# Attention in a fused kernel: the value sums with the values as weights, and the probabilities divided before they are transposed

## The chip, the cores and the metric

The kernel runs on one core of a Trainium2 chip. The metric is the device time of one execution in microseconds (us), taken as the median of several executions. A core has five engines that run side by side and wait for each other through semaphores: PE (TensorE, matrix products; its weight loads are a row of their own in the profile, PEld), DVE (VectorE), ACT (ScalarE), POOL (GpSimd) and SP (here only the queue that issues most DMAs). Each engine works through its own list of instructions strictly in order.

## The reference, cut to what matters

Windowed attention over 4 batches, 8 heads, 768 positions and head width 64, followed by a gated feed-forward layer with a spatial mixing matrix. All of it is float32.

```python
for c in range(nc):                      # 24 chunks of 32 queries
    k_full = concat([mem_k, k[l_start:r_end]])   # 8 memory keys and up to 56 neighbours
    v_full = concat([mem_v, v[l_start:r_end]])
    scores = scale * (q_c @ k_full.T)
    scores = scores - max(scores, -1)
    a = exp(scores)
    a = a / (sum(a, -1) + 1e-09)
    out[c] = a @ v_full
x = out.transpose(0, 2, 1, 3).reshape(B, S, H * D)   # 512 features
h = maximum(x @ w_in, 0.0)
u, v = h[..., :512], h[..., 512:]
v_n = (v - mean(v)) / sqrt(var(v) + 1e-06)
v_s = einsum('ts,bsd->btd', w_spatial, v_n) + b_spatial[None, :, None]
return (u * v_s) @ w_out
```

## The kernel before

**Units.** Attention is cut into 24 units. A unit is 128 query positions (four chunks `c` of 32) of one batch, for all eight heads. The heads are held as four pairs `t`; a pair's two heads `r` lie on partitions 0 to 63 and 64 to 127. Each chunk's window is 64 keys wide. One product of a unit is therefore 4 x 4 x 2 = 32 small matmuls, called a burst here; a float32 matmul shows as two LDWEIGHTS and two MATMUL records, so a burst is 64 records of each.

**One unit, step by step** (line numbers are those of the profile):

- `prep` copies the keys into `kmain` (ACT, L375).
- The scores burst writes the PSUM tile `sx` (PE, L388, in the trace `sx<-kmain,q`): weights are 64 rows by 32 queries, and 64 key columns stream through them.
- `softmax`: the maximum (DVE, L441), the subtraction into `p` (DVE, L445), the exponential (ACT, L450), then sum, epsilon and reciprocal into `rec` (DVE, L455 to L458).
- `turn`: four 128x128 transposes of the undivided `p` into PSUM tile `pt` (PE, L472), copied to `pT` (ACT, L475).
- The value burst (PE, L388, `sx<-vmain,pT`): weights are 64 keys by 32 queries of `pT`, and the 64 value columns stream. Queries come out on partitions. It writes the other half of the `sx` tile of the next unit, and from unit 6 on it is issued as one operation with the next unit's scores.
- `norm` multiplies by the reciprocals, out of PSUM, into `xs` (DVE, L424).
- `turn_x`: four 128x128 transposes of `xs` into `xt` (PE, L487), because the feed-forward layer needs features on partitions.
- `high` and `low` split `xt` into two float32r parts in the tile `x` (ACT, L492, and DVE, L496).

**Around it.** `ffn_v` (one 512-wide group for each unit) and `ffn_u` (four 384-wide groups for every three units) take `x` and the prepared `w_in` in 12 matmuls a group, three for each of four chunks `c` of 128 features (L525 to L527). The `w_in` chunks are prepared at the start from 64-bit words by `from_f64`: a load into `big`, two ACT steps (L825, L830), a DVE step (L834, L835), a POOL addition (L840), and a split on ACT (L854) with a subtraction on DVE or POOL (L858). After the last feed-forward group come the spatial and output products (L686), which the change does not touch.

**What sets the order.** `Plan` simulates all operations with costs written in the code, and emits them in the order of their planned starts. Each operation names its engine, its planned cost, the keys it reads and writes, and a rank; among operations that can start equally early the lower rank goes first. Feed-forward groups have the highest ranks, so they fill PE wherever attention is not ready. Rings (`sizes`) limit how many tiles of a kind are alive. So any edit in the attention steps can move instructions on every engine.

## Time and profile before

| quantity | value |
|---|---|
| median of three executions | 379.65 us |
| the three executions | 379.65, 381.89, 379.65 us |
| the profiled execution, its own time | 378.39 us |
| span of the profiled execution (first to last instruction) | 376.2 us |
| busy: PE, PEld | 355.6, 327.8 us |
| busy: DVE, ACT, POOL | 275.0, 188.8, 139.8 us |
| scores burst, 24 units, MATMUL records | 21.5 us busy |
| value burst, 24 units, MATMUL records | 22.8 us busy |
| transposes `pt` and `xt`, 96 matmuls each | 15.5 and 14.5 us busy |

Busy time is the union of an engine's instructions. A row of a timeline gives the start in us, the duration in us, engine, line, operation, what it writes and reads, and in brackets the idle time of the engine just ahead of it with the operation that ended it. Matmuls overlap each other, so the distance between two starts, not the duration, says what one costs.

### The profile page before, as it was taken

What the parts mean: (1) busy time and instruction counts of PE and PEld (TensorE: products, weight loads), DVE (VectorE), ACT (ScalarE), POOL (GpSimd) and SP (SyncE); (2) the same over time, 40 slices, a digit from 0 to 9 for tenths busy, and PEclk for the clock granted to TensorE, in tenths of its full rate; (3) what the DMA queues carried; (4) which work ended last, traced back from release to release, by engine and by line L of the source; (5) the groups of instructions that cost most, each with busy time, mean ns of one, the idle gap of its engine ahead of it and who ended that gap; (6) DMA issues with size and microseconds to landing.
All of it is one profiled execution on the core that took longest, in us unless ns stands there. A gap on an engine that the chain in (4) does not pass through costs nothing.

```text
span 376.2 us, 11734 instructions
## 1 busy us (share of the span) xinstructions
PE 355.6 (95%) x4964; PEld 327.8 (87%) x4964; DVE 275.0 (73%) x470; ACT 188.8 (50%) x336; POOL 139.8 (37%) x143
## 2 busy tenths in 40 slices
PE   1569899999999999999999999999999999999996
PEld 1357698898988988989889899999999999999996
DVE  3887875757767667775498589787858795896694
ACT  3757544554654456354473366327533742553371
POOL 5444652383484088510033195251026002203410
PEclk9969999999999999999999999999999999999999
DMA  8998888888786783865832649204720582140014
GB/s 230 290 233 228 186 250 232 230 234 250 218 237 192 251 232 92 264 212 181 233 142 92 216 142 319 101 0 167 250 89 0 170 257 80 61 144 8 2 44 167
DMA packets 47368, 65.12 MB, mean 173 GB/s; under 512 B 4434, under 2 KB 38866, under 8 KB 47316
## 3 DMA queue, kind: packets, MB, share of 16 engines
q1 hardware_dynamic: 46900, 64.25, 56.4%
q8 instruction: 39, 0.64, 0.7%
q10 hardware_dynamic: 416, 0.13, 0.1%
q14 instruction: 13, 0.11, 0.1%
HBM read 45.49 MB, written 18.87 MB: 171 GB/s over the span
## 4 chain that ended last, share of the span: by engine, by line
PE 91%; DVE 4%; ACT 2%; DMA 1%; issue 1%; SPq 0%; ACTq 0%; DVEq 0%
PE y L686 22%; PE f L686 17%; PE f L525 13%; PE f L526 12%; PE f L527 12%; PE sx L388 10%; PE xt L487 3%; PE pt L472 3%; DMA k<-in_k_dram 1%; DVE st L835 1%; DVE st L834 1%; DVE mx L441 1%; DVE p L445 0%; PE y L680 0%; PE f L680 0%
## 5 line engine op out<-in xcount | busy, mean ns | idle before, releaser
L742 POOL TENSOR_TENSOR ug<-st,ug 128x384 f32<-128x384 f32 x24 | 33.1, 1392 | 97.7 <-DVE st L734 97.7
L686 PE MATMUL y<-wsp,op 128*128 128x384 f32 x288 | 52.6, 336 | 0.0
L686 PEld LDWEIGHTS y<-wsp,op 128*128 128x128 f32 x288 | 50.1, 188 | 0.0
L525 PE MATMUL f<-x,win_h 128*128 128x384 f32 x128 | 46.3, 362 | 0.0
L527 PE MATMUL f<-x,win_h 128*128 128x384 f32 x128 | 43.1, 337 | 0.0
L526 PE MATMUL f<-x,win_l 128*128 128x384 f32 x128 | 43.0, 336 | 0.0
L525 PE MATMUL f<-win_h,x 128*128 128x512 f32 x96 | 41.7, 435 | 0.0
L686 PE MATMUL f<-wsp,op 128*128 128x384 f32 x216 | 40.1, 336 | 0.0
L526 PE MATMUL f<-win_h,x 128*128 128x512 f32 x96 | 38.6, 402 | 1.5 <-DVE x L496 1.5
L664 DVE TENSOR_TENSOR op<-sm,op 128x768 fp32r<-128x768 f32 x32 | 33.4, 1050 | 7.2 <-ACT op L661 6.6
L527 PE MATMUL f<-win_l,x 128*128 128x512 f32 x96 | 38.4, 400 | 0.0
L686 PEld LDWEIGHTS f<-wsp,op 128*128 128x128 f32 x216 | 37.6, 188 | 0.0
L686 PE MATMUL y<-wout,op 128*128 128x256 f32 x288 | 35.7, 280 | 0.0
L424 DVE TENSOR_TENSOR xs<-sx,rec 128x512 f32<-128x512 f32 x24 | 16.5, 689 | 25.8 <-PE sx L388 25.6
L686 PEld LDWEIGHTS y<-wout,op 128*128 128x128 f32 x288 | 34.8, 188 | 0.1
L661 ACT CAST op<-sm 128x768 fp32r<-128x768 f32 x32 | 26.3, 838 | 15.5 <-DVE sm L647 7.7
L571 POOL TENSOR_TENSOR rstd<-ve,mhalf 128x1 f32<-128x1 f32 x24 | 14.6, 610 | 52.2 <-DVE ve L567 51.8
L388 PEld LDWEIGHTS sx<-kmain,q 64*32 64x32 f32 x1536 | 17.5, 110 | 17.1 <-POOL vmain L370 9.5
L388 PE MATMUL sx<-kmain,q 64*32 64x64 f32 x1536 | 21.5, 235 | 10.6 <-ACT kmain L375 8.4
L596 ACT ACTIVATE uo<-f 128x384 f32<-128x384 f32 x32 | 15.6, 491 | 24.5 <-PE f L527 23.0
L370 POOL COPY vmain<-memv 8x1024 f32<-8x1024 f32 x22 | 23.5, 1075 | 10.2 <-PE sx L388 8.5
L686 PE MATMUL f<-wout,op 128*128 128x256 f32 x216 | 27.1, 280 | 0.0
(92 smaller groups left out, 732.8 us busy)
## 6 DMA issues: line engine op xcount, KB each, us to landing
vmain<-in_v_dram SPq DMA_DIRECT2D x48, 128.0 KB
vn_far<-st SPq DMA_DIRECT2D x24, 256.0 KB
u_far<-uo SPq DMA_DIRECT2D x32, 192.0 KB
vr<-vn_far SPq DMA_DIRECT2D x8, 768.0 KB
ug<-u_far SPq DMA_DIRECT2D x16, 384.0 KB
q<-in_q_dram SPq DMA_DIRECT2D x11, 512.0 KB
out_dram<-ot SPq DMA_DIRECT2D x36, 128.0 KB
vmain<-in_v_dram SPq DMA_DIRECT2D x47, 96.0 KB
```

Of the source, the lines that this page charges most:

```text
L370: {"DVE": nc.vector, "POOL": nc.gpsimd}[eng].tensor_copy(to, of)
L388: nc.tensor.matmul(o, w_, m, start=True, stop=True, skip_group_check=True)
L424: nc.vector.tensor_tensor(xs.rearrange("p t r d -> p r t d"), t_["sx", i][:, :, 1], rec.rearrange("p t r -> p r t").unsqueeze(3).broadcast ...
L525: nc.tensor.matmul(o, lh, rh, start=(j == 0), stop=False)
L526: nc.tensor.matmul(o, ll, rh, start=False, stop=False)
L527: nc.tensor.matmul(o, lh, rl, start=False, stop=(j == len(pairs) - 1))
L571: nc.gpsimd.tensor_tensor(a, t_["ve", i], mhalf, op=ALU.pow)
L596: op("ACT", act(HT), lambda: nc.scalar.activation(alloc("uo", i, [P, HT], F32), t_["f", n], AF.Relu), r=[("f", n)], w=[("uo", i)], rank=rank)
L661: nc.scalar.copy(half(0), of())
L664: nc.vector.tensor_tensor(half(1), of(), half(0).bitcast(F32), op=ALU.subtract)
L686: nc.tensor.matmul(o, x, y, start=first and m == 1 and not (seed and bank != "x"), stop=m == 3 * chunks, skip_group_check=True)
L742: nc.gpsimd.tensor_tensor(g, t_[st(x)], g, op=ALU.mult)
```

## The change

The order of the steps of a unit changes, and the roles of the operands in the value burst are swapped.

- `norm` now divides `p` in place, in SBUF, directly after the reciprocals (DVE), and `turn` transposes the divided `p`.
- The value burst becomes `value_sums`, an operation of its own. The 64x64 block of values is the weight, and the 32 columns of `pT` stream. The result has features on partitions and goes into `xt` directly. It is read by `high` and `low` as before.
- `turn_x`, `xs` and their ring are gone. `sx` still takes two PSUM banks, of which half is used; `xt` takes two banks instead of one, and `pt` one buffer instead of two.
- In `xt`, the head pairs with odd `t` (`e = 1`) have their two heads swapped on the partitions (`r ^ e`), so that two row groups that share output partitions write to different banks. To match it, the rows of the odd chunks of `w_in` are loaded as two swapped halves: `from_f64` now issues one DMA for each entry of a list.
- Scores and value sums are separate operations for all units. `value_sums` has the unit's rank plus 9, the ring `st` grows from 9 to 10.

```diff
-    sizes = {"f": 3, "sx": 1, "pt": 2, "xt": 1, "y": 5, "st": 9, "big": 4, "uo": 2, "x": 2, "vm": 3,
-             "q": 2, "k": 2, "kT": 2, "p": 1, "xs": 1, "pT": 1, "vr": 2, "op": 4, "sm": 2, "ug": 6, "ot": 11}
+    sizes = {"f": 3, "sx": 1, "xt": 1, "pt": 1, "y": 5, "st": 10, "big": 4, "uo": 2, "x": 2, "vm": 3,
+             "q": 2, "k": 2, "kT": 2, "p": 1, "pT": 1, "vr": 2, "op": 4, "sm": 2, "ug": 6, "ot": 11}
...
-                for t, c, r, rows in tiles:
-                    mm(sx[c * CH:(c + 1) * CH, r, 1, t], pT[rows, t, c * CH:(c + 1) * CH], vt[rows, t, c])
...
+    def value_sums(i, rank):
...
+        def go():
+            xt = alloc("xt", i, [P, 2, 2, T // 2, UT], F32, psum=True)[:, :, 0]
+            t_["xt", i] = xt
+            pT, vt = t_["pT", i], v_of(i)
+            for u, c, e, r in [(u, c, e, r) for u in range(T // 2) for c in range(UC) for e in range(2) for r in range(2)]:
+                t, rows = 2 * u + e, head_rows[r]
+                mm(xt[head_rows[r ^ e], e, u, c * CH:(c + 1) * CH], vt[rows, t, c], pT[rows, t, c * CH:(c + 1) * CH])
...
+        op("PE", 0.8, go, r=[("pT", i)] + v_keys(i), w=[("xt", i)], rank=rank, tail=0.25)
...
+        def norm():
+            p3 = t_["p", i].rearrange("p t r w -> p (t r) w")
+            nc.vector.tensor_tensor(p3, p3, t_["rec", i].unsqueeze(2).broadcast_to([P, T * 2, WIN]), op=ALU.mult)
...
-            def turn_x():
-                xs = t_["xs", j].rearrange("p t r d -> p t (r d)")
-                a = alloc("xt", j, [P, T, P], F32, psum=True)
-                for t in range(T):
-                    nc.tensor.transpose(a[:, t], xs[:, t], ident)
...
-        load(get, src_.bitcast(U32).rearrange("p (c w) -> p c w", w=2), w=[("big", big)], r=after, rank=load_rank, seq=True)
+        n = P // len(src_)
+        for j, rows in enumerate(src_):
+            load(lambda j=j: (t_[big] if big in t_ else get())[j * n:(j + 1) * n], rows.bitcast(U32).rearrange("p (c w) -> p c w", w=2),
+                 w=[("big", big, j)], r=after, rank=load_rank, seq=True)
...
-        z, zk = from_f64(("win", c, part), w_in[c * P:(c + 1) * P, cols], rank, load_rank, False)
+        z, zk = from_f64(("win", c, part), [w_in[k * D:(k + n) * D, cols] for k, n in ([(2 * c + 1, 1), (2 * c, 1)] if c % 2 else [(2 * c, 2)])], rank, load_rank, False)
```

**What moves on PE in the steady part.** In a row of the instruction order the tile written stands ahead of the arrow, then the streamed operand and the weights; `x32` counts matmuls. This is PE's list before, from the scores burst of unit 6 (the first of the second batch) to the next transposes:

```order
L388 MATMUL sx<-kmain_144,q 32x64 x32
L388 MATMUL sx<-vmain,pT 32x64 x32
L525 MATMUL f<-win_h,x 128x512
L526 MATMUL f<-win_h,x 128x512
L527 MATMUL f<-win_l,x 128x512
L525 MATMUL f<-win_h,x 128x512
L526 MATMUL f<-win_h,x 128x512
L527 MATMUL f<-win_l,x 128x512
L487 MATMUL xt<-ident,xs 128x128 x4
```

And the same place now (L503 to L505 are the former L525 to L527, L474 is the former L472):

```order
L388 MATMUL sx<-kmain_141,q 32x64 x32
L474 MATMUL pt<-ident,p 128x128 x4
L503 MATMUL f<-win_h,x 128x512
L504 MATMUL f<-win_h,x 128x512
L505 MATMUL f<-win_l,x 128x512
L503 MATMUL f<-win_h,x 128x512
L504 MATMUL f<-win_h,x 128x512
L505 MATMUL f<-win_l,x 128x512
L388 MATMUL xt<-pT,vmain 64x32 x32
L388 MATMUL sx<-kmain_142,q 32x64 x32
```

The value burst no longer follows a scores burst as one operation, and the second set of transposes is gone. From the value sums of the fourth unit to the end (21 value and 20 scores bursts), the list before has 18 scores and value bursts joined, three value and two scores bursts apart, and two sets of transposes for each unit. Now eight pairs stand next to each other, 13 value and 12 scores bursts stand apart, and there is one set of transposes for each unit. The feed-forward groups between them are the same.

**What moves on PE at the start.** Before, around the end of the first feed-forward group, units 1 and 2:

```order
L527 MATMUL f<-win_l,x 128x512
L388 MATMUL sx<-vmain,pT 32x64 x32
L472 MATMUL pt<-ident,p 128x128 x4
L388 MATMUL sx<-kmain_145,q 32x64 x32
L487 MATMUL xt<-ident,xs 128x128 x4
L388 MATMUL sx<-vmain,pT 32x64 x32
L525 MATMUL f<-win_h,x 128x512
```

Now, between the second and the third feed-forward group:

```order
L504 MATMUL f<-win_h,x 128x512
L505 MATMUL f<-win_l,x 128x512
L474 MATMUL pt<-ident,p 128x128 x4
L388 MATMUL xt<-pT,vmain 64x32 x32
L503 MATMUL f<-win_h,x 128x512
L504 MATMUL f<-win_h,x 128x512
L505 MATMUL f<-win_l,x 128x512
```

The transposes and the value burst of unit 2 have moved from ahead of the second group to behind it, and the third group, which reads unit 2's `x`, follows the value burst directly.

**What moves on ACT at that place.** Before, from the copy of unit 2's `pT` on (numbers tell tiles apart; `x_380` written from `xt_604` is unit 2's high part):

```order
L475 COPY pT_498<-pt_490 128x512
L825 ACTIVATE st_501<-big_313 128x512
L830 ACTIVATE big_313<-big_313 128x512
L492 CAST x_380<-xt_543 128x4x128
L825 ACTIVATE st_595<-big_377 128x512
L830 ACTIVATE big_377<-big_377 128x512
L854 CAST win_h_109<-st_501 128x512
L825 ACTIVATE st_616<-big_384 128x512
L830 ACTIVATE big_384<-big_384 128x512
L492 CAST x_380<-xt_604 128x4x128
```

Now, from the same copy to the same high part, which is written from `xt_569`:

```order
L477 COPY pT_561<-pt_553 128x512
L537 ACTIVATE st_567<-f_535 128x512
L812 ACTIVATE big_367<-big_367 128x512
L807 ACTIVATE st_610<-big_379 128x512
L812 ACTIVATE big_379<-big_379 128x512
L836 CAST win_h_109<-st_527 128x512
L420 CAST x_357<-xt_569 128x2x2x128
```

Five operations stand between the two now, eight before; the copy has moved behind most of the preparation of `w_in`.

More of the change, by code (lines that the diff above doesn't have):

```diff
@@ new lines, in tile_chunked_attention_gmlp, with mm, scores @@
+    head_rows = [slice(r * D, (r + 1) * D) for r in range(2)]
+    def mm(o, w_, m):
+        nc.tensor.matmul(o, w_, m, start=True, stop=True, skip_group_check=True)
+    def scores(i, rank):
+        def go():
+            sx = alloc("sx", i, [P, 2, 2, T, D], F32, psum=True)[:, :, 0]
+            t_["sx", i] = sx
+            tq = q_of(i)
+            kT = kmain[i % NK].rearrange("p t c s -> p t (c s)")
+            for t, c, r in [(t, c, r) for t in range(T) for c in range(UC) for r in range(2)]:
+                mm(sx[c * CH:(c + 1) * CH, r, t], tq[head_rows[r], t, c * CH:(c + 1) * CH],
+                   kT[head_rows[r], t, c * SLOT:c * SLOT + WIN])
+        op("PE", 0.8, go, r=qk_keys(i, "q") + [("kmain", i % NK), ("kmem", i % NK)], w=[("sx", i)], rank=rank, tail=0.25)
@@ new lines, in value_sums, with go, part, high @@
+    def value_sums(i, rank):
+        b, tt = i // UB, i % UB
+        n, o = 2 * b + tt // HU, (tt % HU) * UT
+        def go():
+            xt = alloc("xt", i, [P, 2, 2, T // 2, UT], F32, psum=True)[:, :, 0]
[4 more added lines that the diff above has]
+                mm(xt[head_rows[r ^ e], e, u, c * CH:(c + 1) * CH], vt[rows, t, c], pT[rows, t, c * CH:(c + 1) * CH])
+        def part(l):
+            return t_["x", n][:, l].rearrange("p (u e) m -> p e u m", e=2)[:, :, :, o:o + UT]
+        def high():
+            if ("x", n) not in t_:
+                alloc("x", n, [P, 2, T, HT], F32R)
+            nc.scalar.copy(part(0), t_["xt", i])
+        def low():
+            nc.vector.tensor_tensor(part(1), t_["xt", i], part(0).bitcast(F32), op=ALU.subtract)
+        op("PE", 0.8, go, r=[("pT", i)] + v_keys(i), w=[("xt", i)], rank=rank, tail=0.25)
+        op("ACT", act(512) - 0.04, high, r=[("xt", i)], w=[("x", n, tt, "h")], rank=rank)
+        op("DVE", dve(512), low, r=[("xt", i), ("x", n, tt, "h")],
+           w=[("x", n, tt, "l"), *(["attended"] if i == NU - 1 else [])], rank=rank)
@@ new lines, in softmax, with turn, go, copy @@
+        op("DVE", dve(512), sub, r=[("sx", i), ("mx", i)], w=[("p", i)], rank=rank)
+        op("ACT", act(512), exp, w=[("p", i)], rank=rank)
+        op("DVE", dve(512) + 0.43, den, r=[("p", i)], w=[("rec", i)], rank=rank, shared=True)
+        op("DVE", dve(512), norm, r=[("rec", i)], w=[("p", i)], rank=rank, shared=True)
+    def turn(i, rank):
+        def go():
+            p = t_["p", i].rearrange("p t r w -> p t (r w)")
+            a = alloc("pt", i, [P, T, P], F32, psum=True)
+            for t in range(T):
+                nc.tensor.transpose(a[:, t], p[:, t], ident)
+        def copy():
+            nc.scalar.copy(alloc("pT", i, [P, T, P], F32), t_["pt", i])
+        op("PE", 0.47, go, r=[("p", i)], w=[("pt", i)], rank=rank, tail=0.25)
+        op("ACT", act(512) - 0.04, copy, r=[("pt", i)], w=[("pT", i)], rank=rank)
@@ L970, in tile_chunked_attention_gmlp @@
         spread_keys(j, 1.0 + j)
[L971 to L972 removed]
+    for i in range(NU):
+        attend(i, 10.0 * i)
         if i == 0:
```

107 lines of the change are left out of this document (19 added, 88 removed).

## Prediction

> **What bounds the kernel now.** I read the page first, from it the busy shares and the chain of work that ended last:
>
> ```profile
> span 376.2 us, 11734 instructions
> PE 355.6 (95%) x4964; PEld 327.8 (87%) x4964; DVE 275.0 (73%) x470; ACT 188.8 (50%) x336; POOL 139.8 (37%) x143
> PEclk9969999999999999999999999999999999999999
> PE 91%; DVE 4%; ACT 2%; DMA 1%; issue 1%; SPq 0%; ACTq 0%; DVEq 0%
> ```
>
> PE is busy 95% of the span and carries 91% of the chain; its granted clock is full but for the third slice. So the first question is where PE is idle. The windows (stretch, its length, busy time of each engine with the count of records, granted clock, DMA share, GB/s) tell it:
>
> ```profile
> 0.00:20.00 20.00, 7.49 (x204) 5.32 (x204) 12.75 (x22) 10.48 (x18) 10.48 (x16) 1.00 0.98 264
> 20.00:30.00 10.00, 7.19 (x116) 5.46 (x116) 7.64 (x16) 5.24 (x10) 2.91 (x2) 0.66 0.97 238
> 30.00:40.00 10.00, 7.99 (x203) 5.98 (x188) 9.11 (x16) 8.19 (x15) 5.86 (x6) 1.00 0.81 221
> 40.00:80.00 40.00, 39.97 (x816) 35.11 (x815) 28.99 (x60) 20.31 (x37) 20.17 (x22) 1.00 0.83 220
> ```
>
> From 40 us to the last products PE never stops, whatever DVE, ACT or DMA do. There, the time changes only by what PE itself has to execute. PE is idle for 376.2 - 355.6 = 20.6 us; 12.5 + 2.8 + 2.0 = 17.3 of them lie ahead of 40 us, where units 0 to 2 run as a chain over all engines, and the rest at the end. So the sum has two terms: PE work removed or added after the start, at its full price, and the shift of the moment from which PE no longer stops.
>
> **Term 1: PE in the steady part.** What an attention step costs there is not its busy time but the delay of the feed-forward matmuls around it. In the timeline, one set of transposes:
>
> ```profile
> 44.12 0.33 PE L526 MATMUL f<-x,win_l 128*128 128x384 f32 x1
> 44.29 0.34 PE L527 MATMUL f<-x,win_h 128*128 128x384 f32 x1
> 44.47 0.60 PE L487 MATMUL xt<-ident,xs 128*128 128x128 f32 x4
> 44.82 0.42 PE L525 MATMUL f<-x,win_h 128*128 128x384 f32 x1
> 45.08 0.34 PE L526 MATMUL f<-x,win_l 128*128 128x384 f32 x1
> ```
>
> Two 384-wide starts are normally 0.17 apart. From 44.29 to 45.08 are 0.79 for two of them: the transposes cost 0.79 - 0.34 = 0.45 us. A value burst alone, and one joined with scores:
>
> ```profile
> 41.50 0.40 PE L527 MATMUL f<-win_l,x 128*128 128x512 f32 x1
> 41.82 0.86 PE L388 MATMUL sx<-vmain,pT 64*32 64x64 f32 x64
> 42.61 0.50 PE L525 MATMUL f<-win_h,x 128*128 128x512 f32 x1
> 42.95 0.39 PE L526 MATMUL f<-win_h,x 128*128 128x512 f32 x1
> ...
> 56.91 0.40 PE L526 MATMUL f<-win_h,x 128*128 128x512 f32 x1
> 57.14 0.40 PE L527 MATMUL f<-win_l,x 128*128 128x512 f32 x1
> 57.47 0.86 PE L388 MATMUL sx<-kmain,q 64*32 64x64 f32 x64
> 58.13 0.96 PE L388 MATMUL sx<-vmain,pT 64*32 64x64 f32 x64
> 59.35 0.40 PE L526 MATMUL f<-win_h,x 128*128 128x512 f32 x1
> ```
>
> Two 512-wide starts are 0.23 apart. Alone: 42.95 - 41.50 - 0.46 = 0.99 us. Joined: 59.35 - 57.14 - 0.46 = 1.75 us. The joined bursts are not all alike; in the chain of work the 18 last from 1.54 (the first) to 1.70 us (the longest):
>
> ```profile
> 57.54 1.54 PE sx L388 x104
> ...
> 170.02 1.70 PE sx L388 x103
> ```
>
> Six of the 18 take 1.66 to 1.70, so the mean is 0.04 above the first: 1.79 us with the delay around it. Joining saves 2 x 0.99 - 1.79 = 0.19 us.
>
> *Removed*: 21 sets of transposes of the result (units 3 to 23), 21 x 0.45 = 9.4 us. *Given back*: instead of 18 joined pairs there are eight, by the instruction order; 10 x 0.19 = 1.9 us. That is -7.5 us in all.
>
> *Swapped operands*: the value burst keeps 32 matmuls, 64 passes, but its shape changes, and no row of this trace has the new one. Bounds come from how the old one runs. Its weight loads and matmuls (minimum, median, maximum ns; first and last start), and its timeline cut off 0.25 us after its start:
>
> ```profile
> L388 PEld LDWEIGHTS sx<-vmain,pT x64: 102/106/107, 41.8 to 42.4; 64*32 64x32 f32 x64
> L388 PE MATMUL sx<-vmain,pT x64: 212/216/240, 41.8 to 42.5; 64*32 64x64 f32 x64
> ```
>
> ```profile
> 41.82 0.45 PE L388 MATMUL sx<-vmain,pT 64*32 64x64 f32 x32
> ```
>
> Thirty-two passes start in 0.25 us, 7.8 ns apart. Eight array tiles (two row groups, four column groups of 32) take turns, so one tile starts a pass every 62 ns. The stream explains most of that: the transposes above stream 128 columns each and cost 0.45 / 4 = 0.11 us, 0.88 ns a column, 56 ns for 64 columns and 28 for 32. And a weight load grows with its columns:
>
> ```profile
> L686 PEld LDWEIGHTS y<-wsp,op 128*128 128x128 f32 x288 | 50.1, 188 | 0.0
> ```
>
> From 106 ns for 32 columns to 188 for 128 it is (188 - 106) / 96 = 0.85 ns a column as well: 27 ns for 32, 54 for 64. Load and stream together would be 83 ns a pass; at 62 the load is hidden behind the stream. The second half of the burst runs slower than the tiles could: the burst ends at 42.68 (41.82 + 0.86), so its last matmul, of 216 ns, started at 42.46, 0.64 us after the first; the next matmul follows 0.15 later.
>
> New, a pass loads 64 columns (54 ns) and streams 32 (28 ns), on four tiles (two row groups, two column groups of 64). Three values for the burst, whose old length from its start to the next matmul is 42.61 - 41.82 = 0.79 us:
>
> - Loads hide the streams, a tile is bound by its loads: 64 / 4 x 54 ns = 0.86, plus 0.15, is 1.02 us, 0.23 more than before.
> - Loads are not felt: 64 / 4 x 28 = 0.45 is below the 0.64 that the old burst needs for other reasons, and the cost stays: 0 (at best 0.03 less, a shorter last stream).
> - Load and stream of a tile do not overlap: 64 / 4 x 82 = 1.31, plus 0.15, 0.67 more.
>
> I take 0.23, since the rows show loads and streams of a tile overlapping and a load growing with its columns; both ends stay for the range. 21 x 0.23 = +4.8 us. Term 1 is -7.5 + 4.8 = -2.7 us.
>
> **Term 2: the start.** Here are the groups of units 0 to 2 on PE, and the hops of unit 2's chain on ACT:
>
> ```profile
> 26.46 0.63 PE L526 MATMUL f<-win_h,x 128*128 128x512 f32 x1
> 26.88 0.63 PE L527 MATMUL f<-win_l,x 128*128 128x512 f32 x1
> ...
> 34.01 0.50 PE L525 MATMUL f<-win_h,x 128*128 128x512 f32 x1
> 39.33 0.50 PE L526 MATMUL f<-win_h,x 128*128 128x512 f32 x1 [1.51 <-DVE x L496]
> ...
> 39.90 0.60 PE L472 MATMUL pt<-ident,p 128*128 128x128 f32 x4
> ```
>
> ```profile
> 33.29 0.68 ACT L825 ACTIVATE st<-big 128x512 f32<-128x512 f32 x1
> 33.86 0.67 ACT L830 ACTIVATE big<-big 128x512 uint32<-128x512 uint32 x1
> ...
> 40.59 0.59 ACT L475 COPY pT<-pt 128x512 f32<-128x512 f32 x1 [0.49 <-PE pt L472]
> ```
>
> ```profile
> L492 ACT CAST x<-xt 128x512 fp32r<-128x512 f32 x24 | 14.1, 586 | 19.6 <-PE xt L487 19.6
> L496 DVE TENSOR_TENSOR x<-xt,x 128x512 fp32r<-128x512 f32 x24 | 16.5, 690 | 8.5 <-ACT x L492 8.4
> L858 DVE TENSOR_TENSOR win_l<-st,win_h 128x512 fp32r<-128x512 f32 x4 | 2.7, 676 | 0.3 <-ACT win_h L854 0.3
> ```
>
> Group 1 starts at 34.01; group 2 can't go on before 39.33, after the low part of unit 2. Now the sum, the reciprocals and the division (0.68 by the L858 row, the nearest one with two SBUF operands) stand ahead of a unit's transposes, and the second transposes are gone. For units 0 and 1 I let this cancel. Three of group 0's twelve matmuls move ahead of the scores of unit 2. I let group 0 end at 29.6, as now. Behind it: value burst 1.0, high 0.59, low 0.69, three handovers of 0.1: group 1 at 32.2, 1.8 earlier. Twelve matmuls of 0.23: 34.9. Only then come the transposes of unit 2; copy 0.69 later (39.90 to 40.59), 0.59 long: 36.2. Then ACT is the chain: five operations at 0.57 each (33.29 to 33.86) until 39.0, high, low, handovers: group 2 at 40.3. That is 40.3 - 39.33 = +0.9 us, between -1.5 (a faster group 0: nine matmuls at 0.23 instead of the half-clock 0.43 of 26.46 to 26.88) and +2.5 (DVE, busy 9.1 of 10 us in that stretch, late with the division).
>
> **Edits at nothing.** The division replaces the one into `xs`, one for one, on DVE, which is busy 29 of the 40 us after the start; `p` lives longer by three DVE steps of at most 0.7 us, of the 8 us that a unit has there (57.54 to 170.02 in the chain are 14 units). Were that cover gone, PE would wait for `pT`, six matmuls (1.04 us) behind the transposes in many places; the copy ends 1.28 us after their start (39.90 to 41.18) against 0.45 + 1.04 = 1.49. Four more DMA issues on SP stand ahead of value loads; four such loads take 2.63 us to issue:
>
> ```profile
> 2.88 2.63 SPq L257 DMA_DIRECT2D big<-in_moe_w_in_dram  x4
> ```
>
> The two extra ones ahead of unit 0's values delay them by 1.3 us, and its burst comes only behind the preparation of `w_in`, more than 5 us later; without that cover the start would lose those 1.3 us. One `pt` buffer: its copy is done long before the next set.
>
> **Sum.** -2.7 + 0.9 = -1.8 us on the profiled execution's 378.39 us, whose span of 376.2 shrinks alike; the median of the runs, 379.65, lies 1.26 above that execution. On the median: 377.8 us, 0.5% less.
>
> **Rivals.**
>
> 1. *The loads are not felt* (faster). For it: in the second half of a burst the tiles wait for something else already. Against: four tiles instead of eight leave less to overlap. Price: -7.5 + 0.9 = -6.6, 373.0 us.
> 2. *Load and stream in series* (slower). Against it are the 62 ns a pass above; for it, that no row shows a load longer than its stream. Price: +0.67 x 21 = 14.1, so 14.1 - 7.5 + 0.9 = +7.5, 387 us. It decides from 0.31 us more a burst; above 0.5 the kernel is over 1% slower.
> 3. *The clock drops in the new gap.* The window from 20 to 30 us has a granted clock of 0.66, that is 6.8 us at half, after a stretch in which PE did little. From the end of group 1 (34.9) to 40.3, PE now has one set of transposes and one burst, 1.5 of 5.4 us. If that costs the clock for one such spell, up to 6.8 / 2 = 3.4 us of work is lost, 2.9 where the spell begins inside the gap: -1.8 + 2.9 = +1.1, 380.8 us. Against it: the 1.51 us of idle time before 39.33 did not do it. [...]
> 4. *Joining saves nothing between bursts of two shapes.* Scores have 64x32 tiles, values now 64x64. Then eight joined pairs cost 8 x 0.19 = 1.5 more: -0.3, 379.4 us. [...]
>
> **Chances.** Forecast (0.5% faster, its own range 375.5 to 379.5): 0.36. Rival 1: 0.22. Rival 2: 0.10. Rival 3: 0.20. Rival 4: 0.12. About 1%, 3.8 us, is what a measurement of this kernel can tell from no change. Faster by over 1%: rival 1 and the low end of the forecast, 0.27. Slower by over 1%: rival 2 and rivals 3 and 4 together with a late start, 0.14. Within: 0.59. The range goes from rival 1 with its start 0.5 us better, 372.5, to rivals 3 and 4 together with half a microsecond of start lost, 382.8; rival 2 and the extremes of the start stay outside.
>
> **What would show it.** In the new profile: no L487 group; L388 with `xt<-pT,vmain` 24 x 64 records, loads near 133 ns (106 + 27), and 1.02 us from a value burst to the next matmul (0.79: rival 1; 1.45: rival 2); PE without idle time from 40.3 us on; idle stretches before that of about 0.8 and 3 us; the clock row full after 30 us (a second low spell: rival 3). The prediction is wrong if PE waits in the steady part for `pT`, or if the third group starts outside 37.8 to 41.8 us.

## The result, and the profile after

| | before | after | ratio, 95% |
|---|---|---|---|
| median of the runs | 380.72 us | 384.31 us | 1.0077 (1.0049 to 1.0105) |
| the same, measured again beside other kernels | 380.24 us | 384.93 us | 1.0099 (1.0062 to 1.0136) |
| profiled execution (for after, see below) | 378.39 us, span 376.2 | 383.21 us, span 381.2 | |

The change made the kernel slower: the medians lie 3.6 us apart and the ratio is 0.8% above 1, where 1.8 us less were forecast. The ratios, here and below, leave out executions over 1.5% above the fastest of their kernel, the medians count them. The 384.31 us lie above the forecast's range, which ended at 382.8; the kernel before itself took 1.1 us more here than the 379.65 that the forecast started from.

The first profiled execution after the change can't be compared with anything. It took 1902 us. Its page and costliest group (line, shapes, count, busy us, mean ns of one):

```profile
span 1900.3 us, 11575 instructions
PE 1884.0 (99%) x4868; PEld 1608.3 (85%) x4868; DVE 271.8 (14%) x470; ACT 190.1 (10%) x336; POOL 137.0 (7%) x143
L664 PE MATMUL y<-wsp,op 128*128 128x384 f32 x288 | 291.6, 1365 | 0.0
```

DVE and ACT are busy as long as always, but PE's busy time is 5.3 times that of the next profile, and one product takes it 1365 ns, four times the 336 there, with the granted clock shown as full (1.00). No other run did that, and its cause stays open. All that follows uses another execution of the same kernel (383.21 us; a run of the kernel before beside it took 379.25). Its page:

```profile
span 381.2 us, 11575 instructions
PE 356.2 (93%) x4868; PEld 325.3 (85%) x4868; DVE 280.4 (74%) x470; ACT 188.1 (49%) x336; POOL 141.9 (37%) x143
PEclk9999699999999999999999999999999999999999
PE 88%; DMA 9%; DVE 1%; issue 1%; SPq 0%; ACT 0%; DVEq 0%
```

PE is busy as long as before (356.2 against 355.6 us), the span is 5.0 us longer: the time was lost in idling. The chain now has 9% of DMA, 1% before. The low digit of the clock has moved from the third to the fifth slice (38 to 48 us). The windows say the same (columns as in the prediction):

```profile
0.00:20.00 20.00, 5.89 (x138) 4.08 (x138) 12.31 (x23) 10.43 (x17) 10.57 (x16) 1.00 0.97 216
20.00:30.00 10.00, 7.82 (x139) 6.00 (x140) 6.78 (x13) 4.80 (x8) 2.18 (x3) 1.00 1.01 245
30.00:40.00 10.00, 8.05 (x212) 6.13 (x210) 7.77 (x15) 6.73 (x13) 3.57 (x4) 0.98 0.95 203
40.00:80.00 40.00, 36.90 (x743) 30.98 (x744) 30.67 (x60) 18.27 (x33) 17.16 (x21) 0.92 0.76 210
```

From 40 to 80 us PE, which never stopped there before, idles for 3.1 us. But the delay begins earlier. PE's timeline shows it (idle time ahead and what ended it in brackets), around unit 0's value burst and around the third feed-forward group; then come three rows of ACT, ACT's waits for one transfer (us in all, times, longest), and SP's issues:

```profile
17.10 2.07 PE L518 MATMUL f<-win_h 128*128 128x512 f32 x4 [2.61 <-ACT win_h L836]
19.25 0.39 PE L388 MATMUL xt<-pT,vmain 64*64 64x32 f32 x2
20.41 1.93 PE L388 MATMUL xt<-pT,vmain 64*64 64x32 f32 x62 [0.77 <-DMA vmain<-in_v_dram]
...
37.81 1.00 PE L388 MATMUL xt<-pT,vmain 64*64 64x32 f32 x48 [1.14 <-ACT pT L477]
39.27 0.49 PE L388 MATMUL xt<-pT,vmain 64*64 64x32 f32 x16 [0.46 <-issue]
40.99 0.80 PE L503 MATMUL f<-win_h,x 128*128 128x512 f32 x1 [1.22 <-ACT x L420]
42.78 0.79 PE L504 MATMUL f<-win_h,x 128*128 128x512 f32 x1 [0.99 <-DVE x L423]
...
47.05 0.33 PE L503 MATMUL f<-x,win_h 128*128 128x384 f32 x1
```

```profile
12.76 0.67 ACT L807 ACTIVATE st<-big 128x512 f32<-128x512 f32 x1 [1.09 <-DMA big<-in_moe_w_in_dram]
14.84 0.67 ACT L807 ACTIVATE st<-big 128x512 f32<-128x512 f32 x1 [0.84 <-DMA big<-in_moe_w_in_dram]
...
36.62 0.66 ACT L807 ACTIVATE st<-big 128x512 f32<-128x512 f32 x1 [2.34 <-DMA big<-in_moe_w_in_dram]
```

```profile
ACT st L807 <- DMA big<-in_moe_w_in_dram: 4.9, 4, 2.3
```

```profile
2.87 4.28 SPq L257 DMA_DIRECT2D big<-in_moe_w_in_dram  x6
```

The third feed-forward group goes on with its second matmul at 42.78 us (39.33 before, 40.3 forecast), then at half clock until 46.35, and the first 384-wide matmul behind it stands at 47.05 instead of 43.41: 3.6 of the 5.0 us. ACT waits 4.9 us for `w_in`, for which it never waited before. Two of these waits, 1.09 and 0.84 us, stand ahead of the `win_h` that PE needs for the four matmuls at 17.10 (15.37 before). Unit 0's value burst stands behind these four in PE's list, and then waits 0.77 us more for its values. A wait of 2.34 us stands right ahead of the copy of unit 2's `pT`. Behind 47.05 us another 1.4 us are lost on balance. From there to 226 us PE has only four idle times of over 0.1 us, 1.7 us in all. The longest, in the middle of a burst:

```profile
66.79 0.64 PE L388 MATMUL sx<-kmain,q 64*32 64x64 f32 x39 [1.11 <-issue]
```

"issue" means that PE waited for nothing that the profile shows.

### The profile page after: what moved, and what is told of

Same layout as the page of the kernel before. It is cut to its first block, busy times and chain, and to the rows that moved or that the text cites. A ratio compares the mean times of both kernels' runs of the same rounds, so it can differ in the third digit from the quotient of the medians.

```text
span 1900.3 us, 11575 instructions
## 1 busy us (share of the span) xinstructions
PE 1884.0 (99%) x4868; PEld 1608.3 (85%) x4868; DVE 271.8 (14%) x470; ACT 190.1 (10%) x336; POOL 137.0 (7%) x143
## 4 chain that ended last, share of the span: by engine, by line
PE 99%; DMA 0%; DVE 0%; ACT 0%; issue 0%; SPq 0%; ACTq 0%
PE y L664 25%; PE f L664 19%; PE f L503 14%; PE f L504 14%; PE f L505 13%; PE xt L388 6%; PE pt L474 3%; PE sx L388 3%; PE y L658 0%; PE f L658 0%; PE f L518 0%; DMA k<-in_k_dram 0%; ACT x L420 0%; ACT kmain L375 0%; DVE p L443 0%
## 5 line engine op out<-in xcount | busy, mean ns | idle before, releaser
L664 PE MATMUL y<-wsp,op 128*128 128x384 f32 x288 | 291.6, 1365 | 0.0
L664 PEld LDWEIGHTS y<-wsp,op 128*128 128x128 f32 x288 | 261.4, 916 | 23.6 <-issue 23.6
L664 PE MATMUL f<-wsp,op 128*128 128x384 f32 x216 | 219.8, 1362 | 0.0
L664 PEld LDWEIGHTS f<-wsp,op 128*128 128x128 f32 x216 | 195.3, 911 | 18.1 <-issue 18.1
L664 PEld LDWEIGHTS y<-wout,op 128*128 128x128 f32 x288 | 194.7, 938 | 0.4 <-issue 0.4
L664 PE MATMUL y<-wout,op 128*128 128x256 f32 x288 | 194.5, 1030 | 0.0
L503 PE MATMUL f<-x,win_h 128*128 128x384 f32 x128 | 182.1, 1423 | 0.0
L505 PE MATMUL f<-x,win_h 128*128 128x384 f32 x128 | 176.1, 1376 | 0.0
L503 PE MATMUL f<-win_h,x 128*128 128x512 f32 x96 | 171.0, 1781 | 1.5 <-ACT x L420 1.5
L504 PE MATMUL f<-win_h,x 128*128 128x512 f32 x96 | 161.6, 1683 | 0.0
L505 PE MATMUL f<-win_l,x 128*128 128x512 f32 x96 | 160.1, 1668 | 0.0
L503 PEld LDWEIGHTS f<-x,win_h 128*128 128x128 f32 x128 | 109.6, 856 | 22.2 <-issue 21.8
L505 PEld LDWEIGHTS f<-x,win_h 128*128 128x128 f32 x128 | 113.2, 884 | 6.7 <-issue 6.7
L505 PEld LDWEIGHTS f<-win_l,x 128*128 128x128 f32 x96 | 86.7, 903 | 37.9 <-issue 37.9
L504 PEld LDWEIGHTS f<-win_h,x 128*128 128x128 f32 x96 | 89.9, 937 | 27.9 <-issue 26.5
L503 PEld LDWEIGHTS f<-win_h,x 128*128 128x128 f32 x96 | 80.5, 838 | 37.4 <-issue 34.8
```

The costliest lines, as they stand in the source:

```text
L503: nc.tensor.matmul(o, lh, rh, start=(j == 0), stop=False)
L504: nc.tensor.matmul(o, ll, rh, start=False, stop=False)
L505: nc.tensor.matmul(o, lh, rl, start=False, stop=(j == len(pairs) - 1))
L664: nc.tensor.matmul(o, x, y, start=first and m == 1 and not (seed and bank != "x"), stop=m == 3 * chunks, skip_group_check=True)
```

## Experiments: the changed kernel again, its loads and its bursts

**The changed kernel unaltered.**

> The changed kernel as it is, for a profile at the usual speed of PE (the profiled execution on record ran PE at about a fifth of its pace throughout, in 1900 us). The time should be near 384 us, 3 to 4 us above the kernel before. Theory A (weight loads bound the value burst, as predicted, 1.02 us from the burst to the next matmul, and the loss of about 5 us against the forecast lies ahead of the third feed-forward group): a value burst takes 1.0 to 1.05 us, the third group starts after 43 us, and PE has no idle time behind it. Theory B (load and stream of a tile in series): a value burst takes 1.4 to 1.5 us and the third group starts near 40 us. Theory C (PE waits in the steady part for the transposed probabilities): the burst takes 1.0 us, the third group starts near 40 us, and PE has 4 to 6 us of idle time between there and 230 us.

Measured: 383.21 us, the profile above. A value burst, alone and joined with scores, in the timeline, and its weight loads:

```profile
57.62 0.34 PE L505 MATMUL f<-x,win_h 128*128 128x384 f32 x1
57.89 1.13 PE L388 MATMUL xt<-pT,vmain 64*64 64x32 f32 x64
58.96 0.45 PE L503 MATMUL f<-x,win_h 128*128 128x384 f32 x1
59.24 0.34 PE L504 MATMUL f<-x,win_l 128*128 128x384 f32 x1
```

```profile
48.91 0.34 PE L505 MATMUL f<-x,win_h 128*128 128x384 f32 x1
49.18 0.86 PE L388 MATMUL sx<-kmain,q 64*32 64x64 f32 x64
49.96 1.13 PE L388 MATMUL xt<-pT,vmain 64*64 64x32 f32 x64
51.03 0.44 PE L503 MATMUL f<-x,win_h 128*128 128x384 f32 x1
51.31 0.34 PE L504 MATMUL f<-x,win_l 128*128 128x384 f32 x1
```

```profile
L388 PEld LDWEIGHTS xt<-pT,vmain 64*64 64x64 f32 x1536 | 25.9, 138 | 10.2 <-issue 4.7 <-ACT pT L477 2.1 <-DMA vmain<-in_v_dram 1.7
```

Alone it costs 59.24 - 57.62 - 0.35 = 1.27 us, 0.28 more than before; a load takes 138 ns (133 forecast). The pair costs 51.31 - 48.91 - 0.35 = 2.05 us, and 0.99 + 1.27 - 2.05 = 0.21: joining saves between two tile shapes what it saved between two of one shape. The burst is that of theory A, 1.07 us from its start to the next matmul. The third group goes on a little ahead of A's 43 us, and behind it PE does idle, as A did not expect.

**Whole loads of `w_in`.** The host swaps the head rows of the odd chunks in the array; each chunk is one load again:

```diff
-w_in[k * D:(k + n) * D, cols] for k, n in ([(2 * c + 1, 1), (2 * c, 1)] if c % 2 else [(2 * c, 2)])
+w_in[c * P:(c + 1) * P, cols]
```

> The changed kernel, with the rows of the odd chunks of w_in swapped already in the input array, so that each chunk is one load again (4 DMA issues fewer, whole 128-partition loads). Theory A (the start is late because the split loads of w_in reach ACT late: ACT waited 4.9 us for them in the changed kernel): the second matmul of the third feed-forward group starts at 39.5 to 41 us instead of 42.8, and the time falls by 2 to 4 us, to a ratio of 0.995 to 1.003 against the kernel before. Theory S (the start is late because sum, reciprocals and division now stand ahead of the transposes): that matmul stays at 42 to 43 us and the ratio at 1.006 to 1.010.

Measured: 382.62 us, 1.0054 (1.0009 to 1.0100). That is 1.7 us less than the changed kernel, short of the 2 to 4 expected, and the intervals of the two ratios overlap; the trace decides. ACT has no wait for `w_in` left. Unit 0's value burst and the third group:

```profile
15.70 2.08 PE L518 MATMUL f<-win_h 128*128 128x512 f32 x4 [1.19 <-ACT win_h L836]
17.71 1.93 PE L388 MATMUL xt<-pT,vmain 64*64 64x32 f32 x64
...
39.16 0.79 PE L503 MATMUL f<-win_h,x 128*128 128x512 f32 x1 [1.93 <-ACT x L420]
41.04 0.79 PE L504 MATMUL f<-win_h,x 128*128 128x512 f32 x1 [1.09 <-DVE x L423]
...
45.64 0.33 PE L503 MATMUL f<-x,win_h 128*128 128x384 f32 x1
```

Unit 0's burst starts at 17.71 instead of 19.25 and runs through. The first group ends at 29.5 instead of 30.9, and the first 384-wide matmul comes 47.05 - 45.64 = 1.4 us earlier: the price of the split loads is there in full by the end of the first group. (The wait of 2.34 us ahead of the copy of `pT` adds little: the copy starts 1.11 us behind its transposes there, 0.69 here.) So the split loads are part of the loss, not all of it. What still holds the third group at 41.04 is DVE. ACT makes the high part of unit 2's `x` from 38.52 on, but DVE makes the low part only behind the subtraction of unit 3's scores:

```profile
38.52 0.59 ACT L420 CAST x<-xt 128x512 fp32r<-128x512 f32 x1
39.70 0.69 DVE L443 TENSOR_TENSOR p<-sx,mx 128x512 f32<-128x512 f32 x1 [0.53 <-DVE mx L439]
40.30 0.68 DVE L423 TENSOR_TENSOR x<-xt,x 128x512 fp32r<-128x512 f32 x1
```

**Two tiles instead of four**, each head's values on its own row group and columns (`r` for `r ^ e` in the output rows):

> As e2_whole_loads, but without the swap of heads (r instead of r ^ e, and w_in in its own order): the value burst uses two array tiles instead of four. Theory L (a tile is bound by its 64-column weight loads, about 56 ns a pass): 32 passes for each of two tiles, 1.73 to 1.85 us plus 0.15 to 0.2, so a burst takes 1.9 to 2.05 us from its start to the next matmul instead of 1.065, and the time is 18 to 21 us above e2_whole_loads. Theory I (instructions arrive no faster, whatever the tiles): the burst stays below 1.2 us and the time within 3 us of e2_whole_loads.

**Twice the stream**, the 32 columns broadcast to 64, the second half to unused PSUM:

> The changed kernel with every value matmul streaming its 32 columns of probabilities twice (64 columns), the second copy into the unused half of its PSUM bank. Theory L (the stream is hidden behind the 64-column loads): a pass takes the larger of 54 and 56 ns, the burst stays at 1.05 to 1.15 us, and the time within 2 us of the changed kernel. Theory R (load and stream of a tile in series): 16 x (54 + 56) ns = 1.76 plus 0.15, so 1.9 us a burst and about 17 us more.

Measured: 401.62 us, 1.0558 (1.0513 to 1.0603), and 383.98 us, 1.0076 (1.0025 to 1.0127). Their bursts, each with the next matmul (two tiles first):

```profile
59.80 2.05 PE L388 MATMUL xt<-pT,vmain 64*64 64x32 f32 x64
61.79 0.45 PE L503 MATMUL f<-x,win_h 128*128 128x384 f32 x1
```

```profile
57.45 1.16 PE L388 MATMUL xt<-pT,vmain 64*64 64x64 f32 x64
58.54 0.44 PE L504 MATMUL f<-x,win_h 128*128 128x384 f32 x1
```

Half the tiles make the burst 1.99 us instead of 1.07; twice the stream makes it 1.09. So the passes of a tile set the length, 62 to 68 ns each (1.99 / 32, 1.07 / 16, 1.09 / 16), and the stream does not. That the 64-column load is what takes this time fits, but is not shown: a tile of the old burst took 62 ns a pass as well in the burst's first half, with loads of 32 columns and streams of 64, and no run varies the load alone.

**The kernel before with split loads:**

> The kernel before, with the odd chunks of w_in loaded as two halves of 64 partitions each (in their own order), and nothing else changed. Theory A: ACT waits for w_in, the third feed-forward group goes on at 41 to 43 us instead of 39.3, and the time grows by 1.5 to 3.5 us (ratio 1.004 to 1.009). Theory S: the time stays within 1 us of the kernel before.

Measured: 385.27 us, 1.0126 (1.0041 to 1.0210), more than expected. ACT waits 5.0 us for `w_in` here too, and unit 0's value burst starts at 20.82 instead of 18.66 us. But two stalls of 1.99 and 2.04 us inside bursts (ended at 33.33 and 39.10 us) and 6.8 us of half clock stand in the same stretch, so it is no clean price of the loads.

## Experiments: the clock, and where instructions fall in blocks

The idle times inside bursts have one thing in common. Let PE's records (matmuls, weight loads, its semaphore instructions) be counted from the first, in order of start: each stands where the count is 191 or 192 modulo 256. And the page has a DMA queue (packets, MB, share):

```profile
q8 instruction: 38, 0.62, 0.7%
```

0.62 MB in 38 packets are 16 KB each. PE has 9843 records, 259 for each packet: from these numbers and the 256 of the count, the estimate is that a packet carries a block of 256 of PE's instructions. Each stall ended 2.2 to 3.2 us after such a packet began (for the one that ended at 66.79, at 64.2). The reading, as yet an estimate, is that PE had used up a block of instructions and the next was late. To test it, small matmuls on the identity were put ahead of the first scores, where PE is idle for 7 us; each is four records, and all later ones shift against the blocks:

```diff
+if i == 0:
+    for t, c, r in [(t, c, r) for t in range(4) for c in range(UC) for r in range(2)]:
+        mm(sx[c * CH:(c + 1) * CH, r, t], ident[head_rows[r], 0:CH], ident[head_rows[r], 0:WIN])
```

In the same set the gap ahead of the third group (whole loads) was filled:

```diff
+if j == 0 and n == 2:
+    for _ in range(8):
+        nc.tensor.matmul(o, win_h[:, 0, DH:DH + P], win_h[:, 0, DH:], start=True, stop=True)
```

> The changed kernel with whole loads of w_in, and eight more matmuls of 128x512 (the form of the warming matmuls) that TensorE does while the third feed-forward group waits for its x, at about 37.2 to 39.2 us; they write the group's own PSUM tile, which the group's first matmul then overwrites. Theory C, the clock: without the gap the granted clock stays full from 30 us on; the nine matmuls that went at 0.43 us instead of 0.23 gain 9 x 0.2 = 1.8 us; the first 384-wide matmul after the group goes from 45.64 to about 43.9 us, and the ratio to the kernel before from 1.005 to 1.001 (0.996 to 1.005). Rival R, the half clock is only a name for a group that waits for its data anyway: the group's second matmul still waits for x at 41.0 and the group ends at 45.6, ratio 1.005. On the stalls inside bursts (4.1 us of idle TensorE between 50 and 223 us in the run without the extra matmuls): if they come from the fetching of instructions in blocks of 256, the 16 more instructions may move them by a burst or leave them.

> The kernel with the eight warming matmuls, and 32 small matmuls more (128 records on TensorE, half a block of 256) ahead of the first scores, where TensorE is idle until 6.96 us: every later instruction stands 128 places further on in its block. Theory F, stalls come from fetched blocks that arrive late: the stalls inside bursts stand at other bursts than in the kernel without the shift, their sum between 50 and 223 us differs by 0.5 to 4 us from that kernel's, and the time differs by the same (ratio to the kernel before 0.990 to 1.006). Rival P, the stalls belong to places of the program (a wait that the profile doesn't show): same places, same sum within 0.3 us, same ratio within 0.002.

> As the shift by 128, with 16 small matmuls (64 records, a quarter of a block). Theory F: again other places and another sum of the stalls, between 0 and 4 us, and the time goes with the sum; the three kernels of this shift series together give times that lie on a line of slope about 1 against the sum of their stalls. Rival P: same places and sum as without a shift.

> The kernel before, with the same 32 small matmuls ahead of its first scores. It shows 0.03 us of such stalls between 50 and 223 us. Theory F with chance: its blocks merely stood well, and the shift brings stalls of 0.5 to 4 us at bursts, ratio 1.001 to 1.010. Theory F with structure (S): its bursts stand further apart, so that no block is late wherever it begins; stalls under 0.3 us, ratio 0.998 to 1.002. In the second case the stalls are part of what the change does.

| kernel | us | ratio to before, 95% |
|---|---|---|
| whole loads, gap filled | 384.84 | 1.0129 (1.0071 to 1.0186) |
| the same, shift 128 | 386.30 | 1.0158 (1.0105 to 1.0212) |
| the same, shift 64 | 404.64 | 1.0624 (1.0551 to 1.0697) |
| before, shift 128 | 382.92 | 1.0079 (1.0011 to 1.0147) |

The clock first. The windows from 40 to 50 us, with whole loads and with the gap filled:

```profile
40.00:50.00 10.00, 8.96 (x154) 7.59 (x155) 7.53 (x14) 4.20 (x8) 6.22 (x8) 0.73 0.82 211
```

```profile
40.00:50.00 10.00, 8.66 (x219) 7.27 (x222) 9.19 (x16) 5.24 (x9) 7.34 (x9) 1.00 0.79 186
```

The clock stays full, and from the group's second matmul to the first 384-wide one are 2.6 us instead of 4.6. That one stands at 44.20 instead of 45.64, 1.4 us earlier; the rest of the 2.0 us went to a spell of half clock that this execution had from 22.7 to 29.5 us. In all three kernels with the gap filled the clock is full from 30 to 50 us; in five traces without the filling (the unaltered kernel twice, doubled stream, whole loads, two tiles) it drops between 38.5 and 44.3. Theory C holds for the start. Its ratio does not come: the time is no better, and the stalls are other ones (53.3, 116.7 and 190.3 us are new, 100.1, 129.9, 142.8 and 194.0 gone). The shifts decide for theory F: nothing but 64 or 128 records at a place where PE idles, and the stalls move, always to count 192, with 20 us between the best and the worst. In size F was wrong: 0 to 4 us of stalls were expected, and shift 64 brings 19.5 behind the start, 13.2 more than without a shift, for 18.7 us more of span. The kernel before, shifted by 128, stalls too, as F with chance expected. The longest, with shift 64, and the two of the kernel before, shifted:

```profile
125.53 0.66 PE L388 MATMUL sx<-kmain,q 64*32 64x64 f32 x25 [3.18 <-issue]
```

```profile
34.90 0.43 PE L388 MATMUL sx<-kmain,q 64*32 64x64 f32 x5 [3.65 <-issue]
```

```profile
58.89 0.41 PE L388 MATMUL sx<-vmain,pT 64*32 64x64 f32 x20 [2.63 <-issue]
```

**The rest of the late start, and more shifts.** With whole loads, ACT waited for the first group ahead of unit 2's exponential, whose input had been ready since 27.94 us:

```profile
29.55 0.60 ACT L537 ACTIVATE st<-f 128x512 f32<-128x512 f32 x1 [2.27 <-PE f L505]
30.04 0.62 ACT L448 ACTIVATE p<-p 128x512 f32<-128x512 f32 x1
```

One edit puts the exponential first:

```diff
-op("ACT", act(512), relu, r=[("f", n)], w=[k_], rank=rank)
+op("ACT", act(512), relu, r=[("f", n)], w=[k_], rank=rank, after=exps[2] if n == 0 else None)
```

> The changed kernel with whole loads of w_in, in which ScalarE does the exponential of unit 2 ahead of the activation of the first feed-forward group (with whole loads alone it stood behind: ScalarE waited 2.27 us for that group, at 27.27 to 29.55 us, with unit 2's scores ready since 27.94). Theory O, the order of ScalarE makes the rest of the late start: the exponential of unit 2 starts at about 28.0 instead of 30.04, its transposes stand inside the second group instead of behind it, the third group's second matmul goes from 41.04 to 39.0 to 39.8 us (39.33 in the kernel before), its clock stays full, and what is left against the kernel before is -1.6 us of the steady part plus the stalls inside bursts: 378 to 379 us without a stall, one more us for each us of stall. Rival W: the group then waits for something else (the low half of x on VectorE, behind the loads' conversion), at 40.3 or later, and the time stays within 1 us of the run with whole loads.

> The kernel with the exponential first, and 48 small matmuls (192 records on TensorE) ahead of the first scores. In all nine traces so far every stall inside the stages of attention stands at record 192 of a block of 256, counted from the first record of TensorE; theory F says the same here (that is, 192 places earlier in the program than without the shift), with a sum of stalls that may be anything from 0 to 10 us; the time less the stalls is that of the kernel without the shift, within 1 us unless a stall of 3 us lowers the clock.

> The kernel before with 16 small matmuls (64 records) ahead of its first scores. With a shift by 128 it took 382.9 us, 1.008 of the kernel before, and showed stalls of 3.65 and 2.63 us. If the kernel before as it is merely stands well in its blocks, this one shows stalls of 1 to 10 us at record 192 and takes 1.003 to 1.03; if its bursts are robust and the shift by 128 was the exception, under 0.5 us and 0.998 to 1.003.

> As the shift by 64, with 48 small matmuls (192 records). Same two expectations: stalls of 1 to 10 us at record 192 and a ratio of 1.003 to 1.03 if the kernel before as it is stands well by chance, under 0.5 us and 0.998 to 1.003 if not. With the shifts of both kernels the times less the stalls can be set against each other: without stalls the changed kernel with whole loads and warming stood at 378.2 us of span, the kernel before at 376.0.

Measured: 392.59 us, 1.0295 (1.0225 to 1.0365); 394.20, 1.0344 (1.0270 to 1.0417); before with shift 64: 381.71, 0.9990 (0.9939 to 1.0041); with 192: 384.37, 1.0078 (1.0039 to 1.0116). The kernel before beside them took 382.96. With the exponential first:

```profile
37.70 0.50 PE L505 MATMUL f<-win_h,x 128*128 128x512 f32 x1 [1.99 <-ACT x L420]
38.42 0.50 PE L506 MATMUL f<-win_h,x 128*128 128x512 f32 x1 [0.22 <-DVE x L423]
...
41.09 0.33 PE L505 MATMUL f<-x,win_h 128*128 128x384 f32 x1
...
162.99 0.63 PE L476 MATMUL pt<-ident,p 128*128 128x128 f32 x4 [1.39 <-DVE p L462]
```

Theory O holds for the start: the exponential begins at 28.21, the third group goes on at 38.42 (39.0 to 39.8 expected), and the first 384-wide matmul is now 2.3 us earlier than before (41.09 against 43.41), at full clock. The order on DVE has changed as well, so the run shows that the order makes the delay, not that of ACT alone. Nor is the full clock sure: in the five shifted kernels of this order it drops between 35.9 and 42.7 us, and that matmul stands at 42.34 to 47.37. The kernel loses 3%: its stalls add up to 10.6 us. Four more shifts ask whether these are all that it lost.

> The kernel with the exponential first and 8 small matmuls (32 records) ahead of the first scores. Without a shift its third group began its second matmul at 38.42 us and its first 384-wide matmul stood at 41.09 (39.33 and 43.41 in the kernel before), so without stalls it should be 2.3 + 1.6 = 3.9 us faster than the kernel before, a ratio of 0.990. Theory F (the rest is stalls at ends of blocks, and the lower clock that follows long ones): the ratio is 0.990 plus 0.0026 to 0.004 for each us of stall that this trace shows from 30 us on; with a sum of stalls under 3 us it is faster than the kernel before. Rival X (the order of ScalarE costs something else later on): the ratio stays at 1.03 whatever the stalls.

> As with 32 records, with 64 (16 small matmuls): ratio 0.990 plus 0.0026 to 0.004 for each us of stall by theory F, all stalls at record 192 of a block; 1.03 whatever the stalls by rival X.

> As with 32 records, with 96 (24 small matmuls): ratio 0.990 plus 0.0026 to 0.004 for each us of stall by theory F, all stalls at record 192 of a block; 1.03 whatever the stalls by rival X.

> As with 32 records, with 128 (32 small matmuls): ratio 0.990 plus 0.0026 to 0.004 for each us of stall by theory F, all stalls at record 192 of a block; 1.03 whatever the stalls by rival X.

Measured: 394.30, 1.0256 (1.0133 to 1.0379); 386.78, 1.0170 (1.0086 to 1.0255); 387.59, 1.0155 (1.0069 to 1.0241); 390.49, 1.0250 (1.0169 to 1.0330). None beats the kernel before. The second and third lie where theory F puts them by their stalls (1.009 to 1.020, 1.008 to 1.018), the first and fourth above it (1.011 to 1.022, 1.010 to 1.021). Both theories have a part, as the sums below show.

**Once more the changed kernel unaltered.**

> The changed kernel as it is, once more, to see what differs between executions of one program. The earlier look showed five stalls at record 192 of a block (39.3, 66.8, 181.9, 189.1 and 193.2 us; 3.4 us from start to start), a half-clock spell up to 46.35 us and the first 384-wide matmul of the feed-forward product at 47.05. If the place of the instructions alone decides, the stalls stand in the same blocks with the same sum within 0.5 us. If the time at which a block's fetch begins differs from execution to execution, other blocks stall too, or some of these don't, and the sum differs by more; record 192 stays in both cases. Against the kernel before the ratio should be near the 1.0077 measured first.

Measured: 384.93 us. All five stalls stand in the same blocks again, at 39.6, 67.6, 184.0, 191.2 and 195.4 us, each within 0.3 us of its old length, and one is new (120.8 us, 1.43 us). The place of the instructions decides most, but not alone: one execution can add a stall of a microsecond.

The sums, worked out from the traces in us. "First" is the start of the first 384-wide matmul of the feed-forward product; "stalls" the distances of more than 0.33 us between two records at count 191 to 193, behind "first"; "half" the spells of half clock behind it; "rest" is the span less first, stalls and half of "half":

```
kernel                       span   first  stalls       half  rest
before                      376.2   43.41   0  (0)       0    332.8
before, shift 64            377.3   43.01   1.3 (2)      0    333.0
before, shift 128           383.6   47.21   2.9 (1)      0    333.6
before, shift 192           380.8   46.45   1.0 (1)      0    333.4
before, split loads         381.9   48.98   0  (0)       0    333.0
changed                     381.2   47.05   2.7 (4)      0    331.5
changed, again              383.3   47.49   4.4 (5)      0    331.4
changed, doubled stream     382.1   46.53   3.5 (5)      0    332.1
whole loads                 383.1   45.64   5.7 (7)      0    331.7
  two tiles                 400.0   48.00   0.5 (1)      0    351.5
  gap filled                383.0   44.20   6.3 (6)      0    332.5
  gap filled, shift 128     384.0   45.13   5.4 (3)      3.4  331.7
  gap filled, shift 64      401.7   42.75  19.5 (9)     17.1  330.9
  exponential first         388.5   41.09  10.6 (7)      6.8  333.4
    shift 32                386.4   43.06   8.1 (6)      3.4  333.6
    shift 64                382.9   42.34   7.4 (5)      0    333.2
    shift 96                386.1   43.12   7.0 (6)      3.4  334.2
    shift 128               389.7   47.37   4.8 (2)      6.8  334.1
    shift 192               390.4   45.05   9.4 (4)      3.4  334.3
```

The rest hardly depends on the shift: 333.2 on the mean of five kernels with the old value sums, 331.6 of six with the new (changed, whole loads, gap filled), 1.5 us less. With the exponential first it is 333.8; of the 2.2 us, 0.8 to 1.4 are the wait of the row at 162.99, which the new order brings in all six traces, so rival X holds for that much. A long stall often costs more than itself: ten of the sixteen over 2 us go with a spell of half clock of 3.4 us or more. Behind the start the old value sums have stalls of 2.9 us or less in all five traces, the new ones 2.7 or more in thirteen of fourteen. The exception is the kernel with two tiles, whose bursts last twice as long.

The column leaves out the stalls ahead of "first", which can delay it: the kernel before with shift 128 has one of 3.9 us, ended at 34.90, and its "first" is 3.8 us late. With these the kernel before has 0.5 us of stalls as it stands, and 3.9, 6.7, 5.2 and 4.6 in the four rows below it; the changed kernel as it stands has 3.4 and 5.2. So part of the kernel before's lead is luck: it happens to stand well, and its shifts by 128 and 192 cost 0.8%, as much as the change.

The packets bear out this reading of the stalls. Number the packets and the block ends (record 192) in order. Packet n begins around block end n, and by the reading block end n + 1 has to wait for it: at none of the 714 block ends in the nineteen traces does the next record start earlier than 2.2 us after that packet began, and at the 88 that stall it starts 2.2 to 3.2 us after. So a stall comes where a block is used up before its packet has had this time. And the packets begin later with the new value sums: on the mean of a trace, from 43 to 210 us, 1.7 to 2.7 us behind their block end, with the old ones 1.0 to 1.2.

## Why the prediction was wrong

Against the profile before, the span grew by 5.0 us: 3.6 in "first", 2.7 in stalls, -1.3 in the rest. The forecast had +0.9, 0 and -2.7.

- **Edits at nothing, the four more DMA issues.** This step failed. It named the price ("the start would lose those 1.3 us") and the cover, that unit 0's burst comes only behind the preparation of `w_in`. The price was right, 1.4 us, but the cover was not there. Six issues take SP 4.28 us (four took 2.63), and the preparation of `w_in`, which should have hidden this, waits for the split loads itself: PE's first matmuls on `win_h` start at 17.10, with whole loads at 15.70. Unit 0's burst follows 1.5 us late, and waits 0.77 us for its values on top.
- **Rival 3, the clock drops in the new gap**, at 0.20. It happened: filling the gap brought 2.0 us from the third group's second matmul on, 1.4 net, where 2.9 were forecast. It comes on top of the slow start: in both kernels the first group, too, has matmuls at 0.43 us each, until about 29 us. The clock dropped at 39.5 us, after 1.14 and 0.46 us of idling within 3.4 us and no longer gap. The low clock of the kernel before, from which the prediction argued, is weak support: from the first scores to its drop at 22.4 us the longest idle time was 2.87 us, and it ended 7 us ahead of the drop. How much idling brings a drop, no run shows.
- **Term 2, the start**, at +0.9: mis-sized, with the wrong engine at its end. The third group went on at 42.78, outside the 37.8 to 41.8 us that the prediction named as its own test; with whole loads at 41.04, where 40.3 was forecast. The term let ACT bound the chain, and with whole loads ACT is in time: group 0 ends at 29.5 (29.6 forecast) and the high part starts at 38.52 (39.0). But the low part waits for DVE until 40.30, behind the work on unit 3's scores. The upper end of the range had named a late DVE, for the division. With exponential and activation turned round it starts at 37.67, and the group goes on at 38.42.
- **Term 1, the burst.** Its size was 0.28 us instead of 0.23, so the term is -7.5 + 21 x 0.28 = -1.6 us instead of -2.7; the rest in the table fell by 1.3 and 1.4 us in the two traces of the changed kernel, 1.5 on the means. That a tile is bound by its passes, and that the stream is hidden, the two tiles and the doubled stream show; that the load's columns are what binds was argued only.
- **Rivals 1, 2 and 4** are refuted: the burst did get longer, by 0.28 us, load and stream are not in series (with twice the stream the burst takes 1.09 us instead of 1.07), and joining saves 0.21 us between two shapes. Rival 4's price was the author's supposition; no run shows a cost of the change of shape, since joining saved 0.19 us between two of one shape.
- **What no step had**: the stalls at the ends of instruction blocks, 2.7 and 4.4 us behind the start in the two traces of the changed kernel. They alone are more than the whole gain of the steady part.

What stays open: why the packets begin later with the new value sums than with the old, and why their delay behind a block end varies from block to block. Nor does any run show the change without stalls.

## What to carry to other kernels

When a kernel issues many tiny matmuls, compare variants at several shifts of the instruction stream (here three places of one kernel took 384.84 to 404.64 us), and look for idle time with no releaser inside a burst before believing a difference of a per cent. A transfer split in two cost its queue a second issue here (six took 4.28 us, four 2.63), and what stood behind it in the queue paid (unit 0's burst waited 0.77 us for its values). Before a delay is called hidden behind other work, check that the other work does not wait for the same transfers. After a planner's reorder, check the start-up order of every engine operation by operation (with whole loads ACT waited 2.27 us for the first group, with unit 2's exponential ready behind it).

## What the runs showed of the hardware

An execution of the changed kernel has 38 instruction packets of 16 KB (0.62 MB) for 9843 records of PE, 259 for each packet, and the stalls inside bursts stand where the count of these records is 191 or 192 modulo 256. That the packets bring PE its instructions in blocks of 256 is the author's estimate from these numbers. A burst of 128 records in 1.07 us can outrun them: in these traces a record behind a block end never started less than 2.2 us after the packet that it had to wait for by this reading began, and where the block before was used up sooner, PE stalled, for up to 3.9 us at one block end and 19.5 us in all in one execution. A second surprise is the execution of 1902 us, in which PE alone was slow, 5.3 times as long busy as in the next profile (1884.0 against 356.2 us).
